# One Strassen step in a spatial product, attention on 64x64 tiles of TensorE, and a list schedule of all engines

## The chip, the cores and the metric

One core of a Trainium2 chip runs the kernel. The metric is device time in microseconds (us), the lower the better. The engines are PE (TensorE, matmuls; its weight loads are shown apart as PEld), DVE (VectorE), ACT (ScalarE), POOL (GpSimd) and SP, which only starts DMAs here. fp32r is a float format that PE takes in one matmul; a matmul of plain fp32 shows in the trace as two matmul instructions.

## What is computed

Linear attention with per-feature decay (4 batches, 8 heads, 768 tokens, 48 features), then a gated mixer with a product over the tokens:

```python
for t in range(S):
    cur = einsum('bhd,bhe->bhde', u[None] * kt, vt)
    y[:, :, t] = einsum('bhd,bhde->bhe', rt, state + cur)
    state = w[None, :, :, None] * state + einsum('bhd,bhe->bhde', kt, vt)
h = maximum(x @ w_in, 0)                      # x: 4 x 768 x 384, w_in: 384 x 1024
u, v = h[..., :512], h[..., 512:]
v_n = (v - mean(v)) / sqrt(var(v) + 1e-6)     # over the 512 features
v_s = einsum('ts,bsd->btd', w_spatial, v_n) + b_spatial[None, :, None]
out = (u * v_s) @ w_out                       # w_out: 512 x 384
```

## The kernel before, in words

**Precision.** Each fp32 operand of the mixer is split into a high and a low fp32r part, and a product is three fp32r matmuls: high·high, high·low, low·high (`mm3`, lines 430 to 432). ACT makes the high part, DVE or POOL the low one.

**Attention.** A batch is six chunks of 128 tokens; each chunk is worked as two halves of 64. `g1` (314) forms the scores in PSUM bank pair `ps` (line 322) and the chunk's two new states beside them (331), both on 64x64 tiles of the PE array. `mid` (341) lays the masked scores over the diagonal `a` (345), carries the state forward on DVE (353 to 361), and has ACT copy the states into block form `sb` with four copies of 64 partitions (338, 339). `g2` (364) forms the chunk's output in `xp` (371): state times r on tiles of 128 rows by 32 columns, then a times v on tiles of 64 rows by 32 columns. `fin` (393) has ACT cast the high part of x (401); the low part comes from PE and ACT for the first seven chunks (414, 415), later from DVE (406). One `g2(i)` and the following `g1(i+1)` stand together: a burst.

**Mixer.** For each batch `moe_v` (6 chunks, 512 columns), `moe_u` (8 tiles, 384 columns), `moe_sp` (8 tiles, the spatial product: 18 matmuls of 128x128 by 384 columns each) and `moe_out` (6 tiles of 12 such matmuls). `moe_sp` adds the bias on DVE (517), multiplies by u on POOL (518), and `split` makes the two parts (184, 185). For the last three output tiles, `moe_out` first sums three of the four feature blocks for all three tiles and then the fourth, so that the last gate is ready when its turn comes. The output goes through two buffers `ob` (545, 546).

**Preparation.** `prep` (272) scales r and k (POOL 283, DVE 284 or DVE 286), and on POOL forms r·k (289), r·k·u (290) and k·decay (293), then DVE reduces (296) and POOL makes the diagonal `a` (305). The weights w_in and w_out come as 64-bit floats and are turned to fp32 parts by `from_f64` (197), five of the ten blocks with matmuls that subtract (228 to 230); three blocks of w_spatial are split with PE as well (252, 256).

**Order.** Everything is issued in the order of the source: hand-written tables (`FIRST`, `ADJ`, `POUR`, `NORM`) say how many mixer steps stand between two bursts and which pieces of weight work are poured between them; `later` puts normalisation and splits a fixed number of steps behind the matmuls. Each engine takes its instructions in that order.

Of the kernel before, what the change touches and what calls it, by code (L numbers as in the profile page):

```python
# [18 lines left out]
P = 128  # L19
# [8 lines left out]
TH = S // 2  # L28
EPS = 1e-6


OK, OV = DM, DM + DM + 16
ROW = OV + H * 64
# [3 lines left out]
def fused_kernel(ctx, tc, rkT, rkvN, wT, uB, w_in, w_sp, b_sp, w_out, out):  # L37
# [16 lines left out]
    NORM = [2, 2, 4, 3, 3, 5]
    POUR = [(1, 4), (2, 6), (2, 5), (1, 5), (2, 4), (1, 2), (1, 6), (3, 12), (3, 13), (4, 5)]
    const = ctx.enter_context(tc.tile_pool(name="const", bufs=1))
    big = ctx.enter_context(tc.tile_pool(name="big", bufs=6))
    ld = ctx.enter_context(tc.tile_pool(name="ld", bufs=3))
    wk = ctx.enter_context(tc.tile_pool(name="wk", bufs=2))
    sm = ctx.enter_context(tc.tile_pool(name="sm", bufs=2))  # L60
    xp_ = ctx.enter_context(tc.tile_pool(name="xp_", bufs=2))
    ps_a = ctx.enter_context(tc.tile_pool(name="ps_a", bufs=1, space=bass.MemoryType.PSUM))
    ps_x = ctx.enter_context(tc.tile_pool(name="ps_x", bufs=1, space=bass.MemoryType.PSUM))
    ps_m = ctx.enter_context(tc.tile_pool(name="ps_m", bufs=4, space=bass.MemoryType.PSUM))

    wt = const.tile([P, NP], F32, name="wt")
    nc.sync.dma_start(out=wt, in_=wT)  # L70
    dmas, raws = {}, {}

    def raw_in(k):

        t = big.tile([P, 1024], U32, name="raw", tag="vn")
        raws["in", k] = t.rearrange("p (n k) -> p n k", k=2)
        src = w_in[k % NK * P:(k % NK + 1) * P, DH * (k < NK):DH * (k < NK) + DH]
        nc.sync.dma_start(out=raws["in", k], in_=src.bitcast(U32).rearrange("p (n k) -> p n k", k=2))

    def raw_out(k):  # L80
        t = sm.tile([P, 2 * DM], U32, name="raw", tag="gt", bufs=5)
        raws["out", k] = t.rearrange("p (n k) -> p n k", k=2)
        src = w_out[k * P:(k + 1) * P, :]
        nc.sync.dma_start(out=raws["out", k], in_=src.bitcast(U32).rearrange("p (n k) -> p n k", k=2))

    def raw_sp(t, j):
        if t == 0:
            w = sm.tile([P, TH], F32, name="wst", tag="u", bufs=8)
        else:
            w = sm.tile([P, TH], F32, name="wst", tag="ob")  # L90
        raws["sp", t, j] = w
        nc.sync.dma_start(out=w, in_=w_sp[j * P:(j + 1) * P, t * TH:(t + 1) * TH])  # L92

    def load_chunk(m, parts="ab"):
        if m >= NM:
            return
        b, c = divmod(m, NC)
        if "a" in parts:
            rk = ld.tile([P, 2, NP, C], F32, name="rk")
            nc.sync.dma_start(out=rk, in_=rkT[b, c])  # L100
            dmas[m] = [rk]
        if "b" in parts:
            rkv = ld.tile([P, ROW], F32, name="rkv")
            nc.sync.dma_start(out=rkv, in_=rkvN[b, c])
            dmas[m].append(rkv)

    tmp = sm.tile([P, 2 * DM], F32, name="tmp", tag="gt", bufs=5)
    load_chunk(0, "a")
    if not DV0:
        raw_in(0)  # L110
    load_chunk(0, "b")
    if DV0:
        raw_in(0)
    ub = const.tile([P, DM], F32, name="ub")
    nc.sync.dma_start(out=ub, in_=uB)
    load_chunk(1, "a")
    raw_in(1)
    load_chunk(1, "b")
    raw_in(2)
    load_chunk(2)  # L120
    for k in range(3, 6):
        raw_in(k)
    q = tmp[:, 0:256].rearrange("p (n c) -> p n c", n=NP)
    zz = tmp[:, 256:320]
    nc.vector.memset(zz, 0.0)
    nc.scalar.activation(out=tmp[:, 320:321], in_=zz[:, 0:1], func=AF.Sqrt)
    eye = const.tile([P, P], F32, name="eye")
    neg = const.tile([P, P], F32R, name="neg")
    tt = const.tile([P, NP, C], F32, name="tt")
    nc.gpsimd.memset(tt[:, :, 64:65], 1.0)  # L130
    for p in range(NP):
        nc.vector.tensor_tensor_scan(out=q[:, p, :], data0=wt[:, p:p + 1].to_broadcast([P, 64]), data1=zz, initial=1.0,
                                     op0=ALU.mult, op1=ALU.add)
    nc.scalar.copy(tt[:, :, 65:C], q[:, :, 0:63])
    nc.vector.reciprocal(out=tt[:, :, 0:64], in_=q)
    w128 = const.tile([P, NP], F32, name="w128")
    nc.vector.tensor_tensor(out=w128, in0=q[:, :, 63], in1=q[:, :, 63], op=ALU.mult)

    nc.gpsimd.memset(eye, 0.0)
    nc.gpsimd.affine_select(out=eye, in_=eye, pattern=[[-1, P]], compare_op=ALU.not_equal, fill=1.0, base=0,
                            channel_multiplier=1)
    diag = const.tile([P, HC], F32, name="diag")
    nc.gpsimd.tensor_tensor(out=diag, in0=eye[:, 0:64], in1=eye[:, 64:P], op=ALU.add)
# [4 lines left out]
    nc.gpsimd.affine_select(out=mask[0:64], in_=mask[0:64], pattern=[[1, 64]], compare_op=ALU.is_gt,  # L150
                            fill=0.0, base=0, channel_multiplier=-1)
    nc.scalar.mul(neg, eye, -1.0)
    mask_u = mask.bitcast(U32)
    tn = const.tile([P, NP, 2, D], F32, name="tn")
    for p in range(NP):
        pt = ps_m.tile([P, 512], F32, name="pm")
        nc.tensor.transpose(pt[:, 0:P], tt[:, p, :], eye)
        nc.scalar.copy(tn[:, p, :, :], pt[:, 0:P].rearrange("s (j d) -> s j d", j=2)[:, :, 0:D])
    tn_f = tn.rearrange("s p j d -> s (p j d)")

    atiles = []
    for n in range(2):
        t = const.tile([P, 2, NP, HC], F32, name=f"a{n}")
        nc.gpsimd.memset(t, 0.0)
        atiles.append(t)
    sblk = []
    for n in range(2):
        t = const.tile([P, NP, 2 * D], F32, name=f"sb{n}")  # L170
        nc.gpsimd.memset(t, 0.0)
        sblk.append(t)


    wi_h = const.tile([P, NK, DFF], F32R, name="wi_h")
    wi_l = const.tile([P, NK, DFF], F32R, name="wi_l")
    ws_h = const.tile([P, NS, S], F32R, name="ws_h")
    ws_l = const.tile([P, NS, S], F32R, name="ws_l")
    wo_h = const.tile([P, ND, DM], F32R, name="wo_h")
    wo_l = const.tile([P, ND, DM], F32R, name="wo_l")  # L180
    bb = const.tile([P, S], F32, name="bb")

    def split(hi, lo, src, eng=None):
        nc.scalar.copy(hi, src)  # L184
        (eng or nc.vector).tensor_tensor(out=lo, in0=src, in1=hi.bitcast(F32), op=ALU.subtract)  # L185

    casts, rests = [], []

    def flush():
        while rests:  # L190
            rests.pop(0)()

    def cast():
        while casts:
            casts.pop(0)()

    def from_f64(key, hi_w, lo_w, n):


        on_pe = key[1] + 2 * NK * (key[0] == "out") in WPE  # L200
        z = {}

        def first():
            z["pb"] = ps_m.tile([P, 512], F32, name="pm")[:, 0:n].bitcast(U32)
            nc.vector.tensor_scalar(out=z["pb"], in0=raws[key][:, :, 1], scalar1=3, scalar2=0x3FFFFFF8,
                                    op0=ALU.logical_shift_left, op1=ALU.bitwise_and)

        def high():
            z["hb"] = hb = wk.tile([P, 512], U32, name="hb")[:, 0:n]
            nc.vector.scalar_tensor_tensor(out=hb, in0=raws[key][:, :, 1], scalar=0xC0000000, in1=z["pb"],  # L210
                                           op0=ALU.bitwise_and, op1=ALU.bitwise_or)
            if on_pe:
                nc.scalar.copy(hi_w, hb.bitcast(F32))

        def power():
            nc.vector.tensor_scalar(out=z["pb"], in0=z["hb"], scalar1=0xFF800000, scalar2=None, op0=ALU.bitwise_and)

        def low():
# [28 lines left out]
    def sp_pieces(t, j):  # L247
# [17 lines left out]
        return [f]  # L265

    at = {}  # L270

# [444 lines left out]
```

## Time and profile before

| | before |
|---|---|
| three runs, us | 372.51, 374.0, 374.26 (median 374.0) |
| profiled execution | span 370.1 us; the page gives no total of its own |
| PE, DVE, ACT, POOL busy | 340.5, 200.9, 148.2, 159.2 us |
| matmul instructions | 5479 |
| from HBM, to HBM | 36.18 MB, 4.72 MB |

The span runs from the first to the last instruction; a run is some 2.4 to 4.2 us longer. A matmul's row shows its own duration, pipelined with its neighbours: what it costs the stream is the distance from its start to the next one's start.

### The profile page before, as it was taken

How to read it: one execution, taken by the hardware profiler on the slowest of the kernel's cores; microseconds unless marked ns; L12 is line 12 of the kernel's file. 1: busy time of each engine (PE TensorE's matmuls, PEld its weight loads, DVE VectorE, ACT ScalarE, POOL GpSimd, SP SyncE). 2: the span in 40 equal slices, each digit the busy share in tenths (PEclk: the TensorE clock that was granted, in tenths of full speed). 3: DMA queues.
4: the chain of work that ended last, by engine and by line, in shares of the span. 5: the costliest groups of instructions: out<-in, count | busy, mean ns of one | idle time of the engine just before them, and what ended most of it. 6: DMA issues, size and time to landing. Idle time of an engine off the chain costs nothing.

```text
span 370.1 us, 12305 instructions
## 1 busy us (share of the span) xinstructions
PE 340.5 (92%) x5479; PEld 310.8 (84%) x5479; DVE 200.9 (54%) x400; ACT 148.2 (40%) x325; POOL 159.2 (43%) x160
## 2 busy tenths in 40 slices
PE   2759599889999999899999999999989999999994
PEld 1438468779999998799999998899989798999994
DVE  7689766869645553464453635787462614433130
ACT  3055558584123234537122335455131336461211
POOL 5976564663545290745636453235443400013120
PEclk9999989999999999999999999999999999999999
DMA  7993945543031340433031341343041010000101
GB/s 254 418 370 140 302 172 175 173 132 104 29 123 72 132 169 25 132 131 132 2 130 66 130 150 48 130 143 119 0 160 37 4 68 3 0 0 2 63 3 64
DMA packets 14021, 41.69 MB, mean 113 GB/s; under 512 B 1680, under 2 KB 6416, under 8 KB 13968
## 3 DMA queue, kind: packets, MB, share of 16 engines
q1 hardware_dynamic: 13968, 40.90, 31.4%
q8 instruction: 43, 0.70, 0.8%
q14 instruction: 10, 0.08, 0.1%
HBM read 36.18 MB, written 4.72 MB: 111 GB/s over the span
## 4 chain that ended last, share of the span: by engine, by line
PE 84%; ACT 4%; DMA 3%; DVE 3%; issue 3%; SPq 1%; POOL 1%; ACTq 0%; DVEq 0%
PE pm L430 22%; PE pm L431 21%; PE pm L432 21%; PE xp L371 10%; PE ps L322 3%; PE ps L331 3%; DMA rkv<-rkvN 2%; DMA wst<-w_sp 1%; PE pm L228 1%; ACT vs L474 1%; SPq L92 1%; ACT vnorm L476 1%; DVE ws_l L185 1%; PE pm L500 1%; PE pm L505 1%
## 5 line engine op out<-in xcount | busy, mean ns | idle before, releaser
L518 POOL TENSOR_TENSOR g<-g,u 128x384 f32<-128x384 f32 x31 | 31.5, 1017 | 115.8 <-DVE g L517 115.8
L430 PE MATMUL pm<-ws_h,vnorm 128*128 128x384 f32 x192 | 64.8, 337 | 0.0
L432 PE MATMUL pm<-ws_h,vnorm 128*128 128x384 f32 x192 | 64.2, 335 | 0.0
L431 PE MATMUL pm<-ws_l,vnorm 128*128 128x384 f32 x192 | 64.2, 334 | 0.0
L184 ACT CAST gt<-g 128x384 fp32r<-128x384 f32 x32 | 16.4, 513 | 88.9 <-POOL g L518 86.9
L185 DVE TENSOR_TENSOR gt<-g,gt 128x384 fp32r<-128x384 f32 x32 | 21.0, 655 | 55.5 <-ACT gt L184 55.5
L305 POOL TENSOR_TENSOR a<-diag,dg 128x512 f32<-128x512 f32 x24 | 25.4, 1059 | 57.0 <-DVE dg L296 44.3
L430 PEld LDWEIGHTS pm<-ws_h,vnorm 128*128 128x128 f32 x192 | 36.0, 188 | 0.3
L431 PEld LDWEIGHTS pm<-ws_l,vnorm 128*128 128x128 f32 x192 | 36.0, 188 | 0.0
L432 PEld LDWEIGHTS pm<-ws_h,vnorm 128*128 128x128 f32 x192 | 36.0, 188 | 0.0
L430 PE MATMUL pm<-wo_h,gt 128*128 128x384 f32 x96 | 32.7, 340 | 0.0
L432 PE MATMUL pm<-wo_h,gt 128*128 128x384 f32 x96 | 32.3, 336 | 0.0
L431 PE MATMUL pm<-wo_l,gt 128*128 128x384 f32 x96 | 32.3, 336 | 0.0
L451 DVE BATCH_NORM_STATS2 q<-vs 128x6 f32<-128x512 f32 x24 | 16.6, 690 | 28.1 <-ACT vs L444 28.1
L430 PE MATMUL pm<-wi_h,xh 128*128 128x512 f32 x72 | 29.3, 407 | 0.0
L431 PE MATMUL pm<-wi_l,xh 128*128 128x512 f32 x72 | 28.9, 402 | 0.0
L432 PE MATMUL pm<-wi_h,xl 128*128 128x512 f32 x72 | 28.8, 399 | 0.1
L517 DVE TENSOR_TENSOR g<-pm,bb 128x384 f32<-128x384 f32 x32 | 17.7, 553 | 18.9 <-PE pm L432 18.8
L331 PE MATMUL ps<-rkv 64*64 64x48 f32 x704 | 17.2, 221 | 10.9 <-issue 7.3
L290 POOL TENSOR_TENSOR rkv<-rkv,ub 128x384 f32<-128x384 f32 x24 | 26.1, 1089 | 1.9
L293 POOL TENSOR_TENSOR rkv<-rkv,tn 128x384 f32<-128x384 f32 x24 | 26.7, 1114 | 0.0
L289 POOL TENSOR_TENSOR rkv<-rkv 128x384 f32<-128x384 f32 x24 | 25.5, 1062 | 2.3 <-DMA rkv<-rkvN 2.3
(112 smaller groups left out, 725.0 us busy)
## 6 DMA issues: line engine op xcount, KB each, us to landing
rkv<-rkvN SPq DMA_DIRECT2D x24, 648.0 KB, 5.9
rk<-rkT SPq DMA_DIRECT2D x24, 512.0 KB, 4.0
out<-ob SPq DMA_DIRECT2D x24, 192.0 KB, 1.9
raw<-w_in SPq DMA_DIRECT2D x6, 512.0 KB, 9.9
wst<-w_sp SPq DMA_DIRECT2D x12, 192.0 KB, 6.2
raw<-w_out SPq DMA_DIRECT2D x4, 384.0 KB, 6.8
bb<-b_sp SPq DMA_DIRECT2D x1, 384.0 KB, 5.6
ub<-uB SPq DMA_DIRECT2D x1, 192.0 KB, 6.6
```

The costliest lines, as they stand in the source:

```text
L185: (eng or nc.vector).tensor_tensor(out=lo, in0=src, in1=hi.bitcast(F32), op=ALU.subtract)
L289: (nc.vector if DV0 and m == 0 else nc.gpsimd).tensor_tensor(out=rn, in0=rn, in1=kn, op=ALU.mult)
L290: nc.gpsimd.tensor_tensor(out=rn, in0=rn, in1=ub, op=ALU.mult)
L293: (nc.vector if DV0 and m == 0 else nc.gpsimd).tensor_tensor(out=kn, in0=kn, in1=tn_f, op=ALU.mult)
L305: nc.gpsimd.tensor_tensor(out=a.rearrange("s j p t -> s (j p) t"), in0=diag.unsqueeze(1).to_broadcast([P, H, HC]), in1=dg.rearrange("s j p ...
L331: nc.tensor.matmul(ps[64 * j:64 * j + 64, s0 // 64, 256 + p * D:256 + (p + 1) * D], t["kn"][s0:s0 + 64, h * D:h * D + 64], t["v"][s0:s0 + ...
L371: nc.tensor.matmul(xp[32 * g:32 * g + 32, z, jt * HC:(jt + 1) * HC], lhsT, rhs, start=(z, g) not in began, stop=True, skip_group_check=Tru ...
L430: nc.tensor.matmul(o, lh, rh, start=first, stop=False)
L431: nc.tensor.matmul(o, lh, rl, start=False, stop=False)
L432: nc.tensor.matmul(o, ll, rh, start=False, stop=last)
L517: nc.vector.tensor_tensor(out=g, in0=pm[:, 0:TH], in1=bb[:, ts_], op=ALU.add)
L518: (nc.vector if (b, t, d) == (B - 1, 1, ND - 1) else nc.gpsimd).tensor_tensor(out=g, in0=g, in1=u, op=ALU.mult)
```

## The change

**Strassen.** For batches 1 to 3 the 768x768 by 768x512 spatial product is cut into 2x2 blocks and done with seven block products. w_spatial is loaded a second time for four block sums T1 to T4 (made once); each batch needs four sums of the normalised rows (S1, S2, V10, S4) and seven high/low splits 768 columns wide; the sums of products are taken by going on in the same PSUM bank, with a DVE addition read out between (E, U2). Batch 0 stays plain.

**Attention on 64x64.** Output features are laid out in six halves of 64. State times r and a times v both run on 64x64 tiles, 24 fp32 matmuls each in a full chunk (12 for state times r in the first chunk of a batch), the two row halves of the array into two PSUM banks. ACT then copies one bank out and DVE adds it to the other before x is split. The block copies into `sb` go away: the state sits in zero-padded rows.

**List schedule.** Each operation is an `Op` with the engines that may do it, a duration written in the source, what it reads and writes, and the buffers it needs. `Plan.run` plays the list through in order of rank and each engine's program is emitted by planned start. SP's DMAs are in the same list. PE's own list may be reordered within a window of 8 operations (later 3). All six blocks of w_in now use the matmul conversion, no block of w_spatial does. For the first seven chunks r·k, k·decay and r·k·u may run on POOL or DVE, in that order. Batch 0's statistics go to ACT. The output tiles need all four gates before they begin.

```diff
-ROW = OV + H * 64
+ROW = OV + 640
...
+    def xsum(m):
+        def mm(bank, half, z, lhsT, rhs):
+            side, jt = (half % 2, half // 2) if half < NP else (half - NP, 2)
+            te.matmul(xp[64 * side:64 * side + 64, bank, z * 192 + jt * HC:z * 192 + (jt + 1) * HC], lhsT, rhs,
+                      start=(bank, side) not in began, stop=True, skip_group_check=True,
+                      tile_position=(64 * bank, 64 * side))
...
+        def f2():
+            for n in range(2):
+                for pair in PAIRS:
+                    for half in pair:
+                        for z, s0, t0 in SUBS:
+                            (p, j), d = HALVES[half][n]
+                            mm(s0 // 64, half, z, V[s0:s0 + 64, o:o + 64], A[s0:s0 + 64, j, p, :])
...
+    def xout(m):
+        op(act(hi - lo, True), lambda: s.copy(slot(cp)[:, lo:hi], xp[:, 0, lo:hi]), r=["xp"], w=[(m, "cp")], bufs=[cp])
+        op(dve(hi - lo), lambda: v.tensor_tensor(out=xp[:, 1, lo:hi], in0=xp[:, 1, lo:hi], in1=slot(cp)[:, lo:hi], op=ALU.add),
+           r=[(m, "cp")], w=["xp"], bufs=[cp])
...
+    def sp_fast(b):
+        tt_(sv["S1"], V[1, 0], V[1, 1], ALU.add, K[1, 0] + K[1, 1], sk["S1"], [vb, sl["S1"]])
+        tt_(sv["S2"], sv["S1"], V[0, 0], ALU.subtract, sk["S1"] + K[0, 0], sk["S2"], [vb, sl["S1"], sl["S2"]])
+        tt_(V[1, 0], V[0, 0], V[1, 0], ALU.subtract, K[0, 0], K[1, 0], [vb])
...
+        for d in range(2):
+            product(b, "P6", A6, "T2", d, pb[d], (b, "pb", d), True, True, MM)
+            op(dve(TH), lambda d=d: v.tensor_tensor(out=slot(u2, d), in0=pms[pb[d].place][:, 0:TH], in1=E(d, 1)(), op=ALU.add),
+               r=[(b, "pb", d), (b, "E", d, 1)], w=[(b, "U2", d)], bufs=[pb[d], e1[d], u2], near=MM["P6", d])
+        for d in range(2):
+            product(b, "P7", A7, "T3", d, pb[d], (b, "pb", d), False, True, MM)
...
+            X = {x: [M[x, 0], M[x, 1]] for x in ("P1", "P2", "P6", "P7", "P4", "P5", "P3")}
+            L += X["P1"] + X["P2"] + X["P6"] + X["P7"] + X["P4"] + U_[1] + O_[0] + X["P5"] + X["P3"]
+        return L, O_[1]
...
+    for _ in range(6):
+        plan.ranks(at)
+        end = plan.run(lambda t: 8 if t < 60 else 3)
...
+    for o in sorted(plan.ops, key=lambda o: (o.start, o.n)):
+        o.fn()
```

Here `product` is nine fp32r matmuls of 128x128 by 384 columns, `gate` is the bias (or E) addition, the multiplication by u and the split, and `HALVES` says which head and column a half of 64 features begins at.

## Rows read from the trace of the kernel before

**Rows 1.** The page's first part: busy us (share of the span) and instructions.

```profile
PE 340.5 (92%) x5479; PEld 310.8 (84%) x5479; DVE 200.9 (54%) x400; ACT 148.2 (40%) x325; POOL 159.2 (43%) x160
```

**Rows 2.** The chain that ended last, its shares of the span by engine.

```profile
PE 84%; ACT 4%; DMA 3%; DVE 3%; issue 3%; SPq 1%; POOL 1%; ACTq 0%; DVEq 0%
```

**Rows 3.** Busy time by stretch: start:end length, busy us (instructions), PEclk, DMA share, GB/s.

```profile
0.00:13.00 13.00, 3.28 (x69) 2.66 (x69) 7.70 (x13) 3.60 (x9) 8.59 (x21) 1.00 0.80 300
13.00:85.00 72.00, 60.06 (x1330) 46.87 (x1327) 55.37 (x111) 42.31 (x94) 46.91 (x42) 0.98 0.63 220
85.00:364.20 279.20, 276.06 (x4082) 260.54 (x4081) 137.87 (x277) 100.84 (x219) 103.70 (x99) 1.00 0.22 76
364.20:370.10 5.90, 1.06 (x7) 0.74 (x5) 0.00 (x0) 1.44 (x3) 0.00 (x0) 0.88 0.28 100
```

**Rows 4.** PE in order of time, a stretch of the spatial product: start us, us.

```profile
90.44 0.33 PE L432 MATMUL pm<-ws_h,vnorm 128*128 128x384 f32 x1
...
105.17 0.33 PE L430 MATMUL pm<-ws_h,vnorm 128*128 128x384 f32 x1
```

**Rows 5.** PE in order of time, one burst of attention and the matmul behind it.

```profile
105.78 0.88 PE L371 MATMUL xp<-rk,sb 128*32 128x64 f32 x48
106.59 0.97 PE L371 MATMUL xp<-a,rkv 64*32 64x64 f32 x64
107.50 0.69 PE L322 MATMUL ps<-rk 64*64 64x64 f32 x32
108.01 0.63 PE L331 MATMUL ps<-rkv 64*64 64x48 f32 x32
108.57 0.44 PE L430 MATMUL pm<-wo_h,gt 128*128 128x384 f32 x1
```

**Rows 6.** Groups by line: one of the spatial product's three lines, then attention's output.

```profile
L430 PE MATMUL pm<-ws_h,vnorm 128*128 128x384 f32 x192 | 64.8, 337 | 0.0
...
L371 PE MATMUL xp<-a,rkv 64*32 64x64 f32 x1536 | 23.8, 224 | 2.6 <-issue 2.6
...
L371 PE MATMUL xp<-rk,sb 128*32 128x64 f32 x1056 | 20.0, 223 | 0.0
```

**Rows 7.** The chain in order of time: weight conversion on PE.

```profile
30.05 0.88 PE pm L228 x2
30.93 0.23 PE pm L229
```

**Rows 8.** The chain in order of time: the first chunk's load and last preparation.

```profile
2.18 6.62 DMA rkv<-rkvN
...
10.93 0.96 POOL rkv L293
```

**Rows 9.** The chain in order of time: the first and last of three stops in mid-kernel.

```profile
150.59 1.18 issue
...
289.90 0.81 issue
```

**Rows 10.** Single lines: durations in ns, min/median/max, first and last start.

```profile
L185 DVE TENSOR_TENSOR gt<-g,gt x32: 557/559/839, 96.2 to 360.8; 128x384 fp32r<-128x384 f32 x32
...
L286 DVE TENSOR_TENSOR rk<-rk,tt x18: 1214/1216/1960, 58.9 to 293.0; 128x1024 f32<-128x1024 f32 x18
...
L481 POOL TENSOR_TENSOR vnorm<-vs,vnorm x12: 1271/1280/1297, 62.8 to 171.4; 128x512 fp32r<-128x512 f32 x12
L481 DVE TENSOR_TENSOR vnorm<-vs,vnorm x12: 682/693/1384, 229.2 to 329.4; 128x512 fp32r<-128x512 f32 x12
```

**Rows 11.** Groups by line: one of four block copies of the state on ACT.

```profile
L338 ACT COPY sb<-t 64x192 f32<-64x192 f32 x20 | 7.1, 353 | 20.5 <-DVE t L353 20.4
```

**Rows 12.** DVE in order of time, the last gate; in brackets the idle time before.

```profile
359.06 0.56 DVE L517 TENSOR_TENSOR g<-pm,bb 128x384 f32<-128x384 f32 x1 [0.25 <-PE pm L432]
...
360.78 0.56 DVE L185 TENSOR_TENSOR gt<-g,gt 128x384 fp32r<-128x384 f32 x1 [0.58 <-ACT gt L184]
```

**Rows 13.** ACT in order of time, the last copy of an output tile.

```profile
366.79 0.48 ACT L545 COPY ob<-pm 128x384 f32<-128x384 f32 x1 [1.49 <-DMA out<-ob]
```

More of the change, by code (lines that the diff above doesn't have):

```diff
@@ new lines, with __init__ @@
+HALVES = pieces()
+PAIRS = ((0, 1), (2, 3), (4, 5))
+class Buf:
+    def __init__(self, kind, name, dt):
+        self.kind, self.name, self.dt, self.place, self.users, self.open, self.tile = kind, name, dt, None, 0, 0, None
+class Op:
+    def __init__(self, n, ways, fn, bufs, nbytes, tiled):
+        self.n, self.ways, self.fn, self.bufs, self.nbytes, self.tiled = n, ways, fn, bufs, nbytes, tiled
+        self.deps, self.succ, self.rank, self.near = [], [], None, None
+        self.start = self.end = None
@@ L107, in fused_kernel @@
[L107 to L120, printed above, removed]
+    NSLOT, NG, NRK, NRKV, NX = 13, 2, 3, 3, 2
+    XPE, DACT, SACT = 8, 8, 1
+    const = ctx.enter_context(tc.tile_pool(name="const", bufs=1))
@@ new lines, in fused_kernel, with slot, q_ @@
+    SHAPES = {"slot": [2 * TH], "g": [TH], "w": [2 * 3 * TH]}
+    def slot(b, half=None):
+        if b.tile is None:
+            b.tile = const.tile([P] + SHAPES[b.kind], b.dt, name=b.name, tag=f"{b.kind}{b.place}")
+        return b.tile if half is None else b.tile[:, half * TH:(half + 1) * TH]
+    v, s, g, te = nc.vector, nc.scalar, nc.gpsimd, nc.tensor
+    tb = buf("slot", "tmp")
+    dma(lambda: nc.sync.dma_start(out=wt, in_=wT), 2048, w=["wt"])
+    def q_(): return slot(tb)[:, 0:256].rearrange("p (n c) -> p n c", n=NP)
@@ new lines, in fused_kernel @@
+    QS = [("q", p) for p in range(NP)]
+    op(("ACT", 0.4, False), lambda: s.copy(tt[:, :, 65:C], q_()[:, :, 0:63]), r=QS, w=["tt2"], bufs=[tb])
+    op(("DVE", 1.75, False), lambda: v.reciprocal(out=tt[:, :, 0:64], in_=q_()), r=QS, w=["tt3"], bufs=[tb])
+    TT = ["tt1", "tt2", "tt3"]
+    op(("DVE", 0.1, False), lambda: v.tensor_tensor(out=w128, in0=q_()[:, :, 63], in1=q_()[:, :, 63], op=ALU.mult),
+       r=QS, w=["w128"], bufs=[tb])
+    op(("POOL", 0.21, False), lambda: g.memset(eye, 0.0), w=["eye"])
@@ new lines, in fused_kernel @@
+    op(("POOL", 0.24, False), lambda: g.affine_select(
+        out=mask[0:64], in_=mask[0:64], pattern=[[1, 64]], compare_op=ALU.is_gt, fill=0.0, base=0,
+        channel_multiplier=-1), w=["mask"])
+    op(("ACT", 0.3, False), lambda: s.mul(neg, eye, -1.0), r=["eye"], w=["neg"])
+    mask_u = mask.bitcast(U32)
+    head = []
+    tp = buf("pm")
+    for p in range(NP):
+        head.append(op(("PE", 0.25, False), lambda p=p: te.transpose(pms[tp.place][:, p * P:(p + 1) * P], tt[:, p, :], eye),
+                       r=["eye"] + TT, w=["tp"], bufs=[tp]))
@@ new lines, in wkeys, with product, f @@
+    def wkeys(x): return [("W", x, y, i) for y in "hl" for i in range(3)]
+    def product(b, name, A, x, dh, pm, pkey, first, last, MM):
+        hv, lv, keys, bufs = A
+        def f():
+            o = pms[pm.place][:, 0:TH]
+            ds_ = slice(dh * P, (dh + 1) * P)
+            h, l = hv(), lv()
+            for i in range(3):
+                mm3(o, h[:, i, ds_], l[:, i, ds_], W(x)[:, 0, i, :], W(x)[:, 1, i, :], first and i == 0, last and i == 2, True)
+        MM[name, dh] = op(("PE", 1.56, False), f, r=keys + wkeys(x), w=[pkey], bufs=[pm, WB[x]] + bufs)
@@ L121, in fused_kernel, with ld_const, attention @@
+    def ld_const(name, t, src, nbytes):
+        dma(lambda: nc.sync.dma_start(out=t, in_=src), nbytes, w=[name])
+    def attention(m):
+        if m == 0:
+            prep(m)
+            scores(m)
+            mid(m)
+        xsum(m)
+        if m + 1 < NM:
+            prep(m + 1)
+            scores(m + 1)
+            mid(m + 1)
+        xout(m)
+    load(0)
+    ld_const("ub", ub, uB, 196608)
+    for k in range(3):
+        raw_in(k)
+    load(1)
     for k in range(3, 6):
         raw_in(k)
-    q = tmp[:, 0:256].rearrange("p (n c) -> p n c", n=NP)
@@ L124, in fused_kernel @@
[L124 to L133, printed above, removed]
@@ L562, in fused_kernel @@
-    steps += last
-    fill = []
-    for k in range(2 * NK):
-        j, o = k % NK, DH * (k < NK)
-        fill.append(from_f64(("in", k), wi_h[:, j, o:o + DH], wi_l[:, j, o:o + DH], DH))
-    fill += [from_f64(("out", k), wo_h[:, k, :], wo_l[:, k, :], DM) for k in range(ND)]
-    def chain(xs):
-        r, y = [], []
-        for x in xs:
-            r += [x[0]] + y[0:1] + [x[1]] + y[1:] + x[2:4]
-            y = x[4:]
-        return r + y
-    spatial = [sum((sp_pieces(t, j) for j in range(NS)), []) for t in range(2)]
@@ L579, in fused_kernel @@
-    fill = chain(fill[0:NK]), chain(fill[NK:2 * NK]), spatial[0], spatial[1], chain(fill[2 * NK:])
-    marks = [sum(len(x) for x in fill[:k + 1]) for k in range(5)]
-    fill = sum(fill, [])
-    def pour(n):
-        for _ in range(max(0, min(n, len(fill)))):
-            if getattr(fill[0], "key", None) and fill[0].key not in raws:
-                return
-            fill.pop(0)()
-    def sp_loads(t):
-        for j in range(NS if t == 0 else 2):
-            raw_sp(t, j)
-        if t == 0:
-            nc.sync.dma_start(out=bb, in_=b_sp)
@@ L664, in fused_kernel @@
-    for _ in range(6):
-        tick()
+    load(2)
+    load(3)
+    for k in range(6):
+        conv_in(k)
+    for m in range(6):
+        if m + 1 > 3:
+            load(m + 1)
+        attention(m)
+        moe_v(0, m)
+    for j in range(6):
+        conv_sp(j)
+    ld_const("bb", bb, b_sp, 393216)
+    for t in range(2):
+        for d in range(ND):
+            moe_u(0, t, d)
+    sp_plain(0)
+    for k in range(ND):
+        conv_out(k)
+    for t in range(2):
+        for i in range(3):
+            moe_out(0, t, i)
@@ new lines, in fused_kernel @@
+    for b in range(1, B):
+        for c in range(NC):
+            if NC * b + c + 1 < NM:
+                load(NC * b + c + 1)
+            attention(NC * b + c)
+        for c in range(NC):
+            moe_v(b, c)
+        if b == 1:
+            for i in range(3):
+                sums_sp(i)
+        for t in range(2):
+            for d in range(ND):
+                moe_u(b, t, d)
+        sp_fast(b)
+        for t in range(2):
+            for i in range(3):
+                moe_out(b, t, i)
@@ new lines, in fused_kernel @@
+    L, tail = mixer(0)
+    rest = [o for o in L if o is not None and o not in order]
+    for b in range(B):
+        if b:
+            L, tail2 = mixer(b)
+            k = L.index(None)
+            rest = L[:k] + tail + L[k + 1:]
+            tail = tail2
+        bursts = [burst(NC * (b + 1) + c) for c in range(NC)] if b + 1 < B else []
+        total = sum(o.ways[0][1] for o in rest)
+        lead = 6.0 if b == 0 else 14.0
+        step = (total + (0 if b + 1 < B else 0) - lead) / max(1, len(bursts))
+        at, k = 0.0, 0
+        for o in rest:
+            while k < len(bursts) and at >= lead + k * step:
+                order += bursts[k]
+                k += 1
+            order.append(o)
+            at += o.ways[0][1]
+        while k < len(bursts):
+            order += bursts[k]
+            k += 1
@@ new lines, in fused_kernel @@
+    order += tail
+    assert len(order) == len(set(order)) == sum(o.ways[0][0] == "PE" for o in plan.ops), (len(order), len(set(order)))
+    plan.pe_list = order
+    at, now = {}, 4.0
+    for o in order:
+        at[o] = now
+        now += o.ways[0][1]
+    best = None
+    for _ in range(6):
+        plan.ranks(at)
+        end = plan.run(lambda t: 8 if t < 60 else 3)
+        if best is None or end < best[0]:
+            best = end, [(o.start, o.end, o.eng, [b.place for b in o.bufs]) for o in plan.ops]
+        at = {o: o.start for o in order}
@@ L668 @@
+    end = best[0]
+    for o, x in zip(plan.ops, best[1]):
+        o.start, o.end, o.eng = x[:3]
+        for b, n in zip(o.bufs, x[3]):
+            b.place = n
+    global PLANNED
+    PLANNED = plan, end, order
+    for o in sorted(plan.ops, key=lambda o: (o.start, o.n)):
+        o.fn()
+PLANNED = None
 def kernel(r, k, v, w, u, moe_w_in, moe_w_spatial, moe_b_spatial, moe_w_out):
```

1157 lines of the change are left out of this document (684 added, 473 removed).

## The prediction

> **What bounds the kernel now.** I read the page's first part first: PE is busy for 92% of the span, DVE for 54%, POOL for 43%, ACT for 40% [rows 1]. The chain that ended last is PE for 84% of its length [rows 2]. A mean over the span hides its stages, so I cut it into four [rows 3]. Up to 13 us PE waits for loads and constants. From 13 to 85 us it is busy for 60.1 of 72 us while DVE, POOL, ACT and the DMAs are all half busy or more: a stage of latencies, 11.9 us of them open. From 85 to 364.2 us PE is idle for 3.1 of 279.2 us, with DVE at 49%, POOL at 37% and DMA at 22%: here an instruction that PE need not run comes off the time. The last 5.9 us are the output's copies and stores. The granted clock is at or near 1.00 throughout, the 2.4 GHz level, so it is no term.
>
> The stops in the middle are three, 0.8 to 1.2 us each, about 3.1 us in all, and the chain calls them issue, that is, with no releaser shown [rows 9].
>
> The sum is made against the profiled span, 370.1 us; the three runs, median 374.0, lie 3.9 us above it, and I carry that 3.9 unchanged.
>
> **Strassen on PE.** The spatial product is 8 tiles of 18 matmuls a batch, 144, and 576 in all, as three lines of 192 [rows 6]. Seven products of two tiles of nine make 126; three batches drop 54. A busy row says 337 ns for one, but they overlap: from 90.44 to 105.17 us there are 85 steps from start to start, 0.173 us each [rows 4]. 54 x 0.173 = **9.4 us off**, all of it behind 85 us. The four block sums of w_spatial never touch PE.
>
> **Attention on PE.** In a full chunk the output now takes 112 matmul instructions, 48 and 64, from 105.78 to 107.50 us: 1.72 us [rows 5]. Twenty-four fp32 products each for state times r and for a times v give 96 instructions. The nearest row is the scores, the same 64x64 tile with 64 columns: 0.51 us for 32, 15.9 ns each with its change of tile shape; the lower bound is a times v on 64x32 tiles, 0.91 us for 64, 14.2 ns [rows 5]. I take 15 ns: 1.44 us, 0.28 us less a chunk, between 0.19 and 0.36. So a quarter fewer rows of code do not give a quarter of the time: the gain is one instruction in seven and two changes of tile shape. Eighteen chunks behind the start: **5.0 us off** (3.4 to 6.5). A batch's first chunk goes from 88 to 72 instructions, about the same gain.
>
> **The start.** PE work there falls by 6 x 0.28 = 1.7 us for attention. The three blocks of w_spatial that PE split cost it, scaled from 512 to 384 columns, 0.66 + 0.17 us each, 2.5 us in all, and the sixth block of w_in adds 0.88 + 2 x 0.23 = 1.3 us [rows 7]. That is 2.9 us less, in a stage where PE is open for a sixth of the time anyhow; I count half, 1.5 us. Before the first burst, the load lands at 8.80 us and POOL does three operations of about 1 us, k·decay last, until 11.89 us [rows 8]; the change puts k·decay second: 1.0 us off. Against that, each chunk's x now passes an ACT copy (0.48 us for a like one [rows 13]) and a DVE addition (0.56 us [rows 12]) before it can be split: 6.2 us over six chunks if nothing covers them. What covers them are the conversions and `moe_u`, and what falls away in front are the block copies of the state on ACT, 0.35 us each [rows 11]. The bigger rkv adds 66 KB a chunk, 0.2 us at the 300 GB/s of the first stretch [rows 3]. Sum: **2.5 us off**, between 8 off (two thirds of the 11.9 us filled) and 6 on.
>
> **Sums beside PE.** Nothing shows a 768-wide operation. From 384 and 512 columns, DVE medians of 559 and 693 ns [rows 10] extend to about 0.96 us; POOL's 1280 ns for 512 with two thirds of that per column gives at most 1.9 us. A Strassen batch adds to DVE, if DVE does it all, four sums (3.8), seven splits for six narrower ones (7 x 0.96 - 6 x 0.69 = 2.6), two E (1.9), four additions of 384 (2.2), and six additions of x (3.3): 13.8 us in a batch of some 70 us, where it is now half busy. That fits with a fifth to spare, and POOL may take part of it. ACT gains six copies of x and longer casts and loses 22 block copies a batch. So the sums cost nothing by volume; the cover is that share of free DVE time.
>
> What can cost is a **turn**. P6 is read out of its bank by DVE before P7 may go on in it, and likewise P1 to P2, P7 to P4, P5 to P3, twice each: 8 turns a batch, 24 in all. Between the two uses of one bank stands the other tile's product, 9 x 0.173 = 1.56 us. DVE answers PE after 0.25 us and takes 0.56 us [rows 12], so 0.75 us is left, and 0.35 us for the wider E. If DVE is inside a scaling of 1.22 us [rows 10] when the bank is ready, PE waits. Ends: 0 and, for an operation of 1.2 us in front each time, about 0.5 us x 24 = 12. The window of three operations lets other work in, so I take nearer the low end: **1.5 us on**.
>
> **Stops and end.** The stops of 3.1 us stand in the state products, which are not changed; PE has 16 instructions fewer a burst, so I take **1.0 us off** (0 to 3.1). At the end, the last three output tiles must wait for all gates. The last gate's DVE work runs from 359.06 to 361.34 us [rows 12]; before, three tiles' sums over three blocks covered it. After: tiles from 361.4, three times 12 x 0.173 = 6.2 us, then 0.2 us, a copy of 0.48 us, and from that copy's end (367.27) to the span's end 2.8 us as now [rows 13]: 371.1 against 370.1. The old wait of that copy for a store, 1.49 us, goes, since tiles end 2.1 us apart. **1.0 us on**.
>
> Sum: 374.0 - 9.4 - 5.0 - 2.5 - 1.0 + 1.5 + 1.0 = **358.6 us**.
>
> **The rivals.** *The vector engines answer late* (slower). The place is the 24 turns. A DVE operation that reads two SBUF operands sometimes takes far longer than its median: 839 for 559 ns, 1960 for 1216, 1384 for 693 [rows 10], so up to 0.7 us is lost beside something else. The change adds about a dozen such operations a batch and puts more on POOL in the same time. If each turn finds DVE in one so held, PE waits about 1.0 us: 24 x 1.0 on 357.1 gives 381 us. It decides from (374.0 - 357.1) / 24 = 0.70 us a turn. For it speaks that the added sums fall into the very stretch with the turns; against it, that the medians lie at the minima, so most are not held, and that DVE is half idle. The Trainium skill (SBUF — State Buffer, Who interferes with whom) says that a DVE instruction with two SBUF inputs and a GpSimd instruction that reads SBUF shut each other out for a whole instruction; by that rule this rival is what a fuller DVE and POOL bring, and the longest rows agree with it, though the medians show it seldom.
>
> *The start fills up* (faster still). One list places all engines with the weight work; if 10 more of the 11.9 us go and the turns cost nothing, 358.6 - 9.5 - 1.5 = 347.6 us. For it: no engine is full from 13 to 85 us [rows 3]. Against: a list built on written durations meets a stage ruled by DMA landings, and x's chain is longer.
>
> *The start gets worse* (still faster). x's copy and addition are exposed in all six chunks: 358.6 + 2.5 + 6 = 367 us; with orders that miss the DMAs on top, some 372.
>
> *The tiles are no cheaper* (the change does not do what it says there): four 64x64 tiles in a round cost as much as eight of 64x32, attention keeps its 1.72 us: about 365 us. Equal tile shapes in the scores speak against it; it stays in the forecast's own range, 351 to 366.
>
> **Chances.** Forecast 0.52, full start 0.22, worse start 0.13, late answers 0.13. A measurement of this kernel tells apart about 0.5%, 1.9 us: all of the first two and most of the third are faster, 0.84; same 0.04; slower 0.12. The range reaches from the full start with attention at its lower bound, 344, to the worse start, 373, and leaves out the late answers.
>
> **What would show it.** Right: spatial groups sum to 522 matmuls; 96 output instructions a chunk in 1.36 to 1.53 us; PE over 95% busy behind the start; DVE about two thirds busy there. Wrong: PE waits named for DVE between products of one bank, over 0.7 us each; PE idle for more than 18 us between 13 and 85 us; DVE or POOL near 90% in the Strassen stretches.

## The result, and the profile after

The changed kernel takes **356.6 us** (median of four runs, 356.05 to 357.43) against 373.3 for the kernel before (four runs): a ratio of 0.955, 95% interval 0.952 to 0.958, so 16.7 us off. The forecast was 358.6. Most runs are 1.7 us longer than their own span, not 2.4 to 4.2, which sets runs against the span of another execution. So the profiled executions stand for runs of some 371.8 and 357.4 us, and the traces below show 14.4 of the 16.7 us.

The first part of the page of the changed kernel, which answers to [rows 1], and the chain's shares, which answer to [rows 2]:

```profile
span 355.7 us, 11456 instructions
...
PE 327.9 (92%) x5030; PEld 298.3 (84%) x5030; DVE 253.1 (71%) x447; ACT 154.4 (43%) x334; POOL 203.1 (57%) x177
...
PE 70%; DVE 17%; ACT 4%; issue 3%; DMA 3%; POOL 2%; SPq 0%; DVEq 0%; ACTq 0%; POOLq 0%
```

PE has 449 matmul instructions and 12.6 us of busy time less, over a span 14.4 us shorter, and still shows 92%. The work has gone to DVE, from 200.9 to 253.1 us, and POOL, from 159.2 to 203.1; DVE's share of the chain rose from 3% to 17%. The stretches, with the columns of [rows 3]:

```profile
0.00:13.00 13.00, 2.21 (x36) 1.68 (x36) 7.12 (x11) 4.47 (x13) 9.31 (x21) 1.00 0.85 293
13.00:85.00 72.00, 64.70 (x1267) 52.76 (x1268) 66.03 (x124) 49.95 (x129) 42.79 (x40) 0.95 0.61 230
85.00:350.00 265.00, 258.61 (x3716) 241.84 (x3716) 179.97 (x314) 99.00 (x190) 151.01 (x118) 1.00 0.26 93
```

Behind the start PE is idle for 6.4 of 265 us (3.1 of 279 before), with DVE at 68%, as foreseen, and POOL at 57%. From 13 to 85 us DVE is now busy for 66.0 of 72 us, 92%, where it was 77%, and PE is idle for 7.3 us, where it was 11.9. In that stretch PE's clock was granted at 0.95 on the mean, where it was 0.98: more of it ran at the lower level, 1.2 GHz. The clock fell behind PE's two longest waits there, 2.8 us up to 31.3 us and 2.3 us up to 67.9 us (0.64 in the 4.7 us behind the first, 0.67 in the 5.1 us behind the second); before, it fell once, behind a stop of 2.6 us (0.70 in 5.6 us).

One burst, PE in order of time, answers to [rows 5]:

```profile
87.53 0.34 PE L484 MATMUL xp<-rk,sba 64*64 64x64 f32 x8
...
88.28 0.88 PE L484 MATMUL xp<-a,rkv 64*64 64x64 f32 x48
88.98 0.65 PE L439 MATMUL ps<-rk 64*64 64x64 f32 x32
89.45 0.63 PE L451 MATMUL ps<-rkv 64*64 64x48 f32 x32
90.01 0.45 PE L669 MATMUL pm<-B,vh 128*128 128x384 f32 x1
```

The output part takes 88.98 - 87.53 = 1.45 us for 96 instructions (1.72 for 112), the whole burst 2.48 us (2.79). Over the work of 17 chunks behind 85 us, stops left out and the longer step from a full-array matmul into a burst counted in, the starts give 44.2 us against 48.0: 3.8 us, less than 17 times 0.31, since some bursts now stand in two parts and have that step twice. PE's waits behind the start, by releaser:

```profile
PE ps L451 <- issue: 1.5, 1, 1.5
PE pm L671 <- DVE gt L769: 1.0, 1, 1.0
PE pm L669 <- DVE slot L845: 0.9, 1, 0.9
...
PE pm L669 <- DVE g L762: 0.4, 1, 0.4
...
PE pm L669 <- DVE slot L855: 0.4, 1, 0.4
```

L845 (E), L762 (the gate's addition) and L855 (U2) are the turns: 1.7 us in all. L769 is the last gate at the end. With the lines left out, PE waits for 6.3 us, where it was 3.1.

### The profile page after: what moved, and what is told of

It is laid out like the page before. It is cut to its first block, busy times and chain, and to the rows that moved or that the text cites. A ratio compares the mean times of both kernels' runs of the same rounds, so it can differ in the third digit from the quotient of the medians.

```text
span 355.7 us, 11456 instructions
## 1 busy us (share of the span) xinstructions
PE 327.9 (92%) x5030; PEld 298.3 (84%) x5030; DVE 253.1 (71%) x447; ACT 154.4 (43%) x334; POOL 203.1 (57%) x177
## 4 chain that ended last, share of the span: by engine, by line
PE 70%; DVE 17%; ACT 4%; issue 3%; DMA 3%; POOL 2%; SPq 0%; DVEq 0%; ACTq 0%; POOLq 0%
PE pm L669 20%; PE pm L671 19%; PE pm L670 19%; PE xp L484 8%; PE ps L439 3%; PE ps L451 2%; DMA rkv<-rkvN 2%; DVE rk L402 2%; DMA wt<-wT 1%; DVE a L462 1%; DVE g L762 1%; DVE S L826 1%; DVE rk L404 1%; DVE vl L781 1%; DVE xp L527 1%
## 5 line engine op out<-in xcount | busy, mean ns | idle before, releaser
L767 POOL TENSOR_TENSOR g<-g,slot 128x384 f32<-128x384 f32 x28 | 34.0, 1223 | 28.9 <-DVE g L762 28.4
L408 POOL TENSOR_TENSOR rkv<-rkv 128x384 f32<-128x384 f32 x24 | 32.1, 1339 | 26.8 <-DMA rkv<-rkvN 26.8
L669 PE MATMUL pm<-B,vh 128*128 128x384 f32 x102 | 35.0, 343 | 1.4 <-DVE slot L845 0.9
L671 PE MATMUL pm<-B,vl 128*128 128x384 f32 x102 | 34.2, 335 | 0.0
L670 PE MATMUL pm<-B,vh 128*128 128x384 f32 x102 | 34.2, 335 | 0.0
L669 PE MATMUL pm<-xh,wi_h 128*128 128x384 f32 x96 | 33.2, 345 | 0.0
L670 PE MATMUL pm<-xl,wi_h 128*128 128x384 f32 x96 | 32.5, 338 | 0.0
L671 PE MATMUL pm<-xh,wi_l 128*128 128x384 f32 x96 | 32.4, 338 | 0.0
L769 DVE TENSOR_TENSOR gt<-g,gt 128x384 fp32r<-128x384 f32 x32 | 26.0, 813 | 4.6 <-ACT gt L768 4.4
L412 POOL TENSOR_TENSOR rkv<-rkv,ub 128x384 f32<-128x384 f32 x24 | 27.8, 1156 | 0.2
L404 DVE TENSOR_TENSOR rk<-rk,tt 128x1024 f32<-128x1024 f32 x17 | 25.3, 1488 | 1.3 <-DMA rk<-rkT 1.3
L669 PE MATMUL pm<-T,vh 128*128 128x384 f32 x72 | 24.9, 346 | 0.7 <-DVE slot L855 0.4
L462 DVE COPY_PREDICATED a<-mask,ps 128x512 f32<-128x512 uint32 x24 | 17.9, 746 | 9.7 <-PE ps L451 5.2
```

The costliest lines, as they stand in the source:

```text
L404: op(dve(1024, True), lambda: v.tensor_tensor(out=rks[rk.place], in0=rks[rk.place], in1=tt.unsqueeze(1).to_broadcast([P, 2, NP, C]), op=AL ...
L408: o.fn = lambda o=o: pick(o.eng).tensor_tensor(out=RN(), in0=RN(), in1=KN(), op=ALU.mult)
L412: o.fn = lambda o=o: pick(o.eng).tensor_tensor(out=RN(), in0=RN(), in1=ub, op=ALU.mult)
L462: op(dve(512), lambda: v.copy_predicated(out=atiles[t["a"].place], mask=mask_u.unsqueeze(1).unsqueeze(1).to_broadcast([P, 2, NP, HC]), dat ...
L669: te.matmul(o, lh, rh, start=first, stop=False, skip_group_check=skip)
L670: te.matmul(o, lh, rl, start=False, stop=False, skip_group_check=skip)
```

## The experiments

Each is an edit of the changed kernel. Ratios are to the kernel before, run on the same chip; the changed kernel's is 0.955, about 0.0027 a microsecond. Where only what an operation emits is edited, the planned order of all engines stays; where the list is planned anew, it says so.

### Strassen taken out (planned anew)

```diff
-        if b == 1:
-            for i in range(3):
-                sums_sp(i)
...
-        sp_fast(b)
+        sp_plain(b)
...
-        if b == 0:
+        if True:
             dk = [(0, 0), (1, 0), (2, 0), (0, 1), (1, 1), (3, 0), (2, 1), (3, 1)]
```

> The changed kernel with the plain spatial product in all four batches (no block sums, no second load of w_spatial; the list is planned anew). If PE's work is what counts, 54 matmuls come back (9.4 us) and the waits at the turns (2.7 us of stops in the changed kernel's trace) go: 363 us, between 361 and 366. If the sums on DVE and POOL had eaten the gain: 358 or less. If Strassen's gain was whole: 366 or more.

367.9 us, ratio 0.984 (0.980 to 0.989). So Strassen is worth 0.029, **11 us give or take 2**: no less than the 9.4 us on PE, and no net price for the turns is seen. A new list alone can move the time by several us (below), but the profiled runs show no such thing here: PE is busy for 9.6 us more than in the changed kernel and idle for 27.8 us in both (365.3 - 337.5 and 355.7 - 327.9). The plain form waits as much for its gates. The page's row of PE, and PE's waits behind the start up to 350 us:

```profile
span 365.3 us, 11443 instructions
...
PE 337.5 (92%) x5084; PEld 307.4 (84%) x5084; DVE 218.6 (60%) x411; ACT 141.8 (39%) x313; POOL 152.0 (42%) x150
...
PE pm L669 <- ACT gt L768: 1.9, 2, 1.0
PE ps L451 <- issue: 0.9, 1, 0.9
PE pm L671 <- DVE gt L769: 0.8, 1, 0.8
...
```

What is left, 0.984 against 1, or 5.8 us (4.3 to 7.4), is attention, the weight conversion and the list together.

### More PE work: short instructions, early and late

The state product is issued twice, in chunks 0 to 5 (first kernel) or 6 to 23 (second):

```diff
-            for pair in PAIRS:
+            for rep in range(2 if m < 6 else 1):
+              began.clear()
+              for pair in PAIRS:
```

> State times r is done twice over in the six chunks of the first batch, with the same result, and the order of every engine as it was: 264 more PE instructions of 16.3 ns, 4.3 us of PE work. If the first 85 us are half open, as the prediction counted, 2 us longer than the changed kernel (0.5 to 3.5): 358.7. If PE is the bound there too, 361; if the stage is open, 356.6.

> The same in the eighteen chunks of batches 1 to 3: 792 more PE instructions, 12.9 us of PE work. If PE sets the end behind the start, all of it comes back: 369.5 us (367.5 to 371). If stops of DVE and POOL cover part of it, under 365.

363.5 us, ratio 0.975 (0.969 to 0.982): 7.5 us more (5 to 10) for 4.3 us of PE work. And 373.1 us, ratio 0.995 (0.991 to 1.000): 15 us more (13 to 17) for 12.9. Both missed on the same side. The price of the work was forecast too high besides: by the starts in the trace the second copy takes 0.70 us in a full chunk, 14.6 ns an instruction for 16.3, so 3.9 and 11.5 us. The waits of the second, behind the start, show a surplus of stops with no releaser, 5.0 us where the changed kernel has 1.9:

```profile
PE ps L451 <- issue: 2.6, 2, 1.8
PE ps L439 <- issue: 2.4, 3, 0.9
...
```

### The same PE time in few long instructions

Full fp32r matmuls of 384 columns ahead of the state product, four in each later chunk (five in chunks 1 to 5 in the second kernel, with another slice of `wi_h`):

```diff
             R = rks[t["rk"].place]
+            for i in range(4 if m >= 6 else 0):
+                te.matmul(xp[:, i % 2, 0:384], wi_h[:, 0, 0:P], wi_h[:, 0, 0:384], start=True, stop=True,
+                          skip_group_check=True)
             for pair in PAIRS:
```

> In the eighteen chunks of batches 1 to 3 four full fp32r matmuls of 384 columns are put ahead of state times r, into a bank that is then overwritten: 72 instructions, 12.5 us of PE work, nearly as much as the doubled state product (12.9 us in 792 instructions, measured some 15 us longer with more stops without a releaser). If those stops belong to the number of instructions, this one costs its 12.5 us and no more: 369 us, with about 2 us of such stops. If any PE time that is added costs a fifth more: 371.5 or more.

> Five full fp32r matmuls of 384 columns ahead of state times r in chunks 1 to 5, into a bank that is then overwritten: 25 instructions, 4.3 us of PE work before 85 us, in the same order of all engines. The same work as 264 short instructions cost some 7 us. If the stage is half open, as the prediction counted: 2 us more than the changed kernel, 358.7. If PE's work there comes back whole: 361. If short instructions were not the reason for the surplus: 363.5.

Late: 366.3 us, ratio 0.981 (0.977 to 0.985), 9.5 us more for 12.5 us of work. Not one stop without a releaser is left behind the start; these are all of PE's waits there but the two for the last gates at the end (0.2 and 1.0 us, as in the changed kernel):

```profile
PE pm L672 <- ACT xh L536: 0.6, 1, 0.6
PE xp L492 <- ACT xl L540: 0.6, 1, 0.6
PE pm L672 <- DVE slot L858: 0.4, 1, 0.4
PE xp L492 <- DVE xl L542: 0.2, 1, 0.2
```

So long instructions cost less than their time, and short ones more. The waits account for most of it: behind the start PE waits for 8.1 us with the short ones, 6.3 in the changed kernel and 3.0 with the long ones, which with the added work makes 13.3 and 9.2 us of the 15 and 9.5. Early: 362.3 us, ratio 0.969 (0.964 to 0.974), 5 us more (3 to 7) for 4.3. By the runs PE work put into the bursts before 85 us comes back whole, not by half. The trace does not say the same of the long ones: by 85 us that kernel's PE is 14 matmuls of 384 columns, 2.4 us, behind the changed kernel's, and kernels with the same start lie up to 8 such matmuls apart. So whole or half is not settled, and work outside the bursts, such as the conversions, was not tested.

### A change of tile shape inside a burst

```diff
             V, A = rkvs[t["rkv"].place], atiles[t["a"].place]
+            te.matmul(ps[:, 0, 448:464], neg, neg[:, 0:16], start=True, stop=True, skip_group_check=True)
```

> Between state times r and a times v one matmul of the full array (16 columns, into unused columns of ps) is put in all 24 chunks: two more changes of tile shape a chunk. In the kernel before, such changes took about 0.15 us each where a short matmul takes 0.015. If they are what the common tile shape saved: 24 x 0.3 = 7 us more, 363.5. If a change costs nothing and the number of instructions alone counts: 357.

361.6 us, ratio 0.967 (0.961 to 0.973): 4.5 us more, give or take 2.5. In the burst (PE in order of time) it takes this:

```profile
90.64 0.30 PE L484 MATMUL xp<-rk,sbb 64*64 64x64 f32 x8
90.87 0.28 PE L506 MATMUL ps<-neg 128*128 128x16 f32 x1
91.07 0.93 PE L484 MATMUL xp<-a,rkv 64*64 64x64 f32 x48
```

From the last group of the state product to a times v it is 0.43 us, where the changed kernel has 88.28 - 88.16 = 0.12. So two changes cost 0.31 us at the place, 7.4 us over 24 chunks, of which some 4.5 reached the end; PE's waits behind the start fell meanwhile from 6.3 to 2.7 us. The changes that the new form saves are between other shapes. There, in the trace of before, the step from the last state product to the first a times v and the step from there to the scores are 0.15 us each, where the other steps are 12 to 14 ns on the mean. So a part of attention's gain is the common tile shape and not the number of instructions.

### All added sums on DVE (planned anew)

```diff
-            o = op([dve(n, True), pool(n)], None, r=r, w=w, bufs=bufs)
+            o = op(dve(n, True), None, r=r, w=w, bufs=bufs)
...
-        o = op([dve(n, True), pool(n)], None, r=keys + [(b, name, "h")], w=[(b, name, "l")], bufs=[hb, lb] + sbufs)
+        o = op([dve(n, True), pool(n)] if b == 0 else dve(n, True), None, r=keys + [(b, name, "h")], w=[(b, name, "l")],
+               bufs=[hb, lb] + sbufs)
```

> The four sums of normalised rows and the seven low parts of batches 1 to 3 are all given to DVE, none to POOL (some 14 us more DVE work, 27 us less POOL work; the list is planned anew). If the sums are hidden by volume: within 2 us of the changed kernel, 355 to 359. If DVE's answers at the turns are what the added work endangers: 361 or more, with PE waits named for DVE in the spatial product of over 6 us.

364.8 us, ratio 0.977 (0.972 to 0.982): 8 us longer. Two waits of PE for DVE's low parts and the stretch around the longer:

```profile
PE pm L671 <- DVE vl L782: 4.3, 2, 4.1
PE xp L484 <- DVE xl L539: 2.3, 1, 2.3
...
160.00:180.00 20.00, 15.94 (x226) 14.94 (x228) 17.84 (x24) 5.13 (x8) 13.90 (x10) 0.83 0.19 69
```

DVE is at 89% in these 20 us and PE at 80%, with the clock at 0.83 behind the stop. In the changed kernel the same stretch has DVE at 76%, POOL at 89% and PE at 98%:

```profile
160.00:180.00 20.00, 19.54 (x380) 18.08 (x382) 15.11 (x23) 5.01 (x9) 17.87 (x13) 1.00 0.31 113
```

The waits are for the very operations that were moved: the sums are not hidden by volume over a batch, since they fall into the 20 us of the products. How much of the 8 us is the new list's is open; a new list alone has cost as much, as the decay weights' load shows.

### The turns further apart (planned anew)

```diff
-            L += X["P1"] + X["P2"] + X["P6"] + X["P7"] + X["P4"] + U_[1] + O_[0] + X["P5"] + X["P3"]
+            L += X["P1"] + X["P6"] + X["P2"] + X["P7"] + U_[1][:1] + X["P4"] + U_[1][1:] + O_[0] + X["P5"] + X["P3"]
```

> PE's list takes the products as P1, P6, P2, P7, one tile of u, P4, so that two products or more stand between two uses of a bank (the list is planned anew). If the turns' stops of 2.7 us count: 1 to 2.5 us less, some 355. If they only stand where PE would wait for the next parts anyway: within 0.7 us; slower than 358 if P6's parts, needed 3 us sooner, come too late.

360.4 us, ratio 0.965 (0.962 to 0.969), 4 us longer. The waits at the same lines are there, and longer:

```profile
PE pm L669 <- DVE g L762: 2.0, 1, 2.0
PE pm L669 <- DVE slot L855: 1.7, 1, 1.7
PE pm L669 <- DVE slot L845: 1.7, 1, 1.7
...
```

More distance between two uses of a bank did not take the waits away. Whether the earlier need of P6's parts or merely the new plan made them longer is open.

### The decay weights loaded first

First planned anew, then with the old list kept (the planned operation stays and emits nothing; only SP's order changes):

```diff
-    dma(lambda: nc.sync.dma_start(out=wt, in_=wT), 2048, w=["wt"])
+    nc.sync.dma_start(out=wt, in_=wT)
...
+    nc.sync.dma_start(out=wt, in_=wT); dma(lambda: None, 2048, w=["wt"])
```

> The small load of the decay weights is issued before all others; in the changed kernel it lands at 5.2 us, behind the first chunk's big loads, and the scores begin at 11.4 us where they began at 7.2 before. If that start is a chain into the end: 1.5 to 4 us less, some 354. If the stage up to 85 us is ruled by the loads and DVE that follow: within 0.7 us, 356.6.

> As the earlier trial with the decay weights loaded first, but with the planned list kept as it is: on every engine the order is the changed kernel's, only SP issues this load ahead of rkv. That trial was 8 us longer although PE had caught up 3 us at 13 us; its mid-kernel stops stood in another planned order. If the start's lead is absorbed by what follows: 356.6 within 0.8. If the lead reaches the end: 353.5 to 355. If issuing it first is itself harmful: over 360.

Planned anew: 364.9 us, ratio 0.977 (0.973 to 0.981), 8 us **longer** with an earlier start. PE's waits from 160 to 200 us in that run:

```profile
PE ps L439 <- DVE a L462: 3.9, 1, 3.9
PE pm L669 <- DVE slot L855: 1.8, 1, 1.8
PE pm L669 <- DVE slot L845: 0.6, 1, 0.6
```

With the list kept: 356.9 us, ratio 0.954 (0.950 to 0.958), no difference. Its first bursts, against 11.36 and 13.45 us in the changed kernel:

```profile
9.94 1.13 PE L439 MATMUL ps<-rk 64*64 64x64 f32 x32 [3.55 <-DVE rk L402]
12.12 1.11 PE L451 MATMUL ps<-rkv 64*64 64x48 f32 x32 [1.06 <-POOL rkv L410]
```

So 1.4 us of lead at the start is absorbed, and the 8 us were the new list's: a small edit to what the planner sees moved stops about in mid-kernel, by more than most of the effects studied here.

### The end

```diff
-            for d in range(d0, d1):
+            ds = (2, 3, 0, 1) if (b, t) == (B - 1, 1) else (0, 1, 2, 3)
+            for d in ds:
...
-                mm3(pms[pm.place][:, 0:DM], h[:, o], l[:, o], wo_h[:, d, :], wo_l[:, d, :], d == 0, d == ND - 1)
+                mm3(pms[pm.place][:, 0:DM], h[:, o], l[:, o], wo_h[:, d, :], wo_l[:, d, :], d == ds[0], d == ds[-1])
```

> The last three output tiles sum the feature blocks in the order 2, 3, 0, 1, so the two gates that come last stand last. In the changed kernel PE stops for 0.4 and 1.2 us there. If those stops are the end's own price: 1.2 us less than the changed kernel (0.5 to 1.6), some 355.4. If the last gate sets the end through the store that follows: no change, 356.6.

> The same load first with the same list, and the last output tiles' sums in the order 2, 3, 0, 1: the sum of both, 355.3 if only the end counts, 352.5 to 354 if both do.

The end alone: 355.3 us, ratio 0.951 (0.947 to 0.955), within what can be told from the changed kernel. With the load first: **354.9 us**, ratio 0.948 (0.944 to 0.952), 2.5 us better than the changed kernel's ratio, give or take 1.8, and the best version run. PE's stop at the last gate is 0.5 us where it was 1.0:

```profile
343.68 0.34 PE L670 MATMUL pm<-wo_l,gt 128*128 128x384 f32 x1
344.50 0.44 PE L671 MATMUL pm<-wo_h,gt 128*128 128x384 f32 x1 [0.49 <-DVE gt L769]
```

## Why the prediction was right, and where a step was not

- **Strassen, 9.4 us off:** right. Taking it out cost 11 us, give or take 2, and 9.6 us of PE's busy time.
- **The turns, 1.5 us on:** the waits named at them are 1.7 us, but as a price the step was not needed, since the plain product waits about as much for its gates. "DVE answers PE after 0.25 us" misread its row: that is DVE's idle time before the operation, which begins 0.04 us behind the end of PE's row (358.68 + 0.34 us).
- **Attention, 0.28 us a chunk:** right for one burst, 0.27 in the output and 0.31 in the whole; with bursts in two parts 3.8 us over 17 chunks, where 4.8 was forecast for as many. That the count of instructions and the changes of tile shape both carry it was right too.
- **The start, 2.5 us off:** the way was right, the size too small and its parts partly wrong. At 85 us both kernels stand at the same chunk of attention, but the changed one has begun 40 of batch 0's spatial matmuls, the kernel before none. The first of three such lines in each, with first and last start, and the same line of the changed kernel from 85 us on:

```profile
L430 PE MATMUL pm<-ws_h,vnorm x192: 333/334/445, 90.0 to 358.3; 128*128 128x384 f32 x192
...
L669 PE MATMUL pm<-B,vh x102: 332/335/447, 75.5 to 343.5; 128*128 128x384 f32 x102
...
L669 PE MATMUL pm<-B,vh 128*128 128x384 f32 x89 | 30.6, 343 | 1.4 <-DVE slot L845 0.9 <-DVE g L762 0.4
```

  It has some more of other work left; in all it is 32 matmuls of 384 columns ahead, 32 x 0.173 = 5.5 us (27 to 35 of them in five other runs of its list). That is 3 us more than was forecast. It would fit if attention's and the conversions' 2.9 us came whole and the fall of PE's idle time from 11.9 to 7.3 us brought the rest, a part of what the rival of the full start saw. The 1.0 us for k·decay in second place did not come: the decay weights' load went behind the chunk's loads, the scores began at 11.36 us and the first states at 13.45, where the last POOL step before ended at 11.89 [rows 8]. Loading them first moved the end by nothing. That x's longer way is exposed is seen twice before 85 us, in the waits of 2.8 and 2.3 us for ACT's cast, and not in every chunk. What limits the stage now is DVE, at 92%, which holds 24 of the 35 us of the chain from 13 to 48 us; "no engine is full" no longer holds there.
- **The sums, nothing by volume:** right for the kernel as written, wrong as reasoned. "If DVE does it all" it does not fit: that run is 8 us longer, in part perhaps by its list. The step took a mean over a batch of 70 us where the demand stands in 20. There POOL is at 89%, which the prediction named as a sign of being wrong, but with PE at 98% it cost nothing.
- **The stops, 1.0 us off:** 1.9 us behind the start where there were 3.1. Not foreseen were 1.6 us of other waits there, for x's parts, the diagonal and low parts, and slower steps of PE in between: its matmuls of 384 columns follow each other by 178 ns on the mean behind 85 us, where it was 175, and those of 512 by 234, where it was 232, 2.7 us in all. What holds them is open; they are too short to show as idle.
- **The end, 1.0 us on:** a hole was there, 0.2 and 1.0 us, of which about half can be had back, but the premise was wrong. An output tile does not wait for all gates; each matmul waits for what it reads. PE in order of time, then DVE's last gate:

```profile
344.37 0.44 PE L669 MATMUL pm<-wo_h,gt 128*128 128x384 f32 x1 [0.23 <-ACT gt L768]
...
345.41 1.22 DVE L769 TENSOR_TENSOR gt<-g,gt 128x384 fp32r<-128x384 f32 x2
```

  The first tile begins at 344.37 us, 2.3 us before the last gate is ready at 346.63. From there to the span's end it is 9.1 us, where it was 8.8, so 0.3 us on.
- **The rival of late answers** did not come in the changed kernel, but it did in the run with all sums on DVE and in the two with other lists. The condition that was named for it, that most operations are not held, has gone weaker. Single lines of the changed kernel:

```profile
L769 DVE TENSOR_TENSOR gt<-g,gt x32: 523/638/1396, 88.9 to 346.1; 128x384 fp32r<-128x384 f32 x32
...
L767 POOL TENSOR_TENSOR g<-g,slot x28: 1002/1020/1996, 85.9 to 327.7; 128x384 f32<-128x384 f32 x28
```

The median of the gate's low part rose from 559 to 638 ns and its longest from 839 to 1396, and a POOL line that never passed 1.03 us now reaches 2.0: some 0.8 and 1.0 us more, about one operation of the other engine. The Trainium skill (SBUF — State Buffer, Who interferes with whom) says that a DVE instruction with two SBUF inputs contends with a GpSimd instruction that reads SBUF; these longest rows agree with it.

The two terms of PE work, 14.4 of 15.4 us, were sized from the steps between starts of like rows, and held. That the sum came within 2 us is also luck: by the two traces the start gave 3 us more than its term, and what follows 85 us took about as much back. There PE's waits are 3.2 us longer and its steps 2.7 us slower, and from PE's last matmul to the span's end it is 1.4 us less: 4.5 us on, where turns, stops and end were forecast at 1.5.

## What to carry to other kernels

Where PE is full, price a matmul by the distance between starts and count instructions and tile shapes, not lines of source. Price moved work on the other engines in the stretch where it falls due, not over the mean of a batch. Before an experiment on a kernel with a planned order is believed, keep the list fixed: planning anew alone moved this one by up to 8 us.

## What was not expected of the hardware

Short instructions cost more than their time. Doubling the state product added 792 of them, 11.5 us by their starts, and 15 us came; 72 long ones, 12.5 us, cost 9.5 and left no stop without a releaser behind the start. One of those stops, in the doubled run, PE in order of time; the instruction DMA queue from 109.5 to 111 us, where the stop begins (110.6); and that queue over the whole run before, in the changed kernel and in the doubled run:

```profile
110.10 0.50 PE L451 MATMUL ps<-rkv 64*64 64x48 f32 x19
112.39 0.44 PE L451 MATMUL ps<-rkv 64*64 64x48 f32 x13 [1.78 <-issue]
...
q8 instruction: 1, 0.02, 5.6%
...
q8 instruction: 43, 0.70, 0.8%
q8 instruction: 39, 0.64, 0.7%
q8 instruction: 45, 0.74, 0.8%
```

A transfer on the instruction queue (16 KB, one of 45 in the run) is under way as PE comes to a stand in the middle of a product, and the stops at 150.6 us before and 155.7 us after have one beside them too. By its count the queue brings PE's code: 43, 39 and 45 transfers stand against 2 x 5479, 2 x 5030 and 2 x 5822 matmuls and weight loads, one for each 255 to 259. Behind 85 us all ten such stops of the three traces begin 1.0 to 2.2 us after a transfer has begun, and there is only one transfer in 8 to 9 us. A burst of 160 matmuls is 320 instructions in 2.5 us, more than one transfer holds; of 384-column matmuls as many as one holds last 22 us. That PE waits there for its own code fits all this; that it is the cause was not shown by taking a transfer away.
